# A gated mix of a two-dimensional spectral filter and a dense GELU layer on one core: output and dense sums in contiguous parts, operands at multiples of 256 bytes, first products reordered, four first folds by transfers, a new table of ranks

## The chip, the core and the metric

The kernel runs on one core of one Trainium2 chip. A core has a matrix engine (TensorE, PE in the profile, its weight loads PEld), a vector engine (VectorE, DVE), a scalar engine (ScalarE, ACT), GpSimd (POOL) and SyncE (SP). Transfers are issued by SP, ACT or POOL and all run on the same 16 DMA engines. The metric is device microseconds of one execution of the program; lower is better.

## The reference

```
x = A_x                                        # [1, 2048, 512] float32
g = sigmoid((x * gate_w).sum(-1))              # a gate for each of 2048 rows
X = rfft2(x) * (A_w_r + 1j * A_w_i)            # 2048 x 257 complex weights
a = irfft2(X)                                  # the spectral branch
h = gelu(x @ B_w1 + B_b1)                      # 512 -> 1792  (the rows of A_x are used for both branches)
b = h @ B_w2 + B_b2                            # 1792 -> 512
out = g * a + (1 - g) * b
```

In the last call of the reference both branches get `A_x`. All is float32.

## The kernel before

**Arithmetic.** Each float32 operand of a product is split into a high and a low part (`split`, L563 to L569: ACT rounds the high part, DVE subtracts it to get the low part), and one product is three matmuls, high by high, high by low, low by high (`prods`, L526). All matmuls, weight loads and transfers of the helpers show under the lines of the helpers: matmuls L524, transfers from POOL that add to their destination L515 (`acc`), plain ones from POOL L511 (`dma_pool`).

**Spectral branch.** The 2048 rows are 16 blocks `j` of 128. `forward(j)` folds the 512 columns into sums and differences (first folds L679, second folds L693), multiplies by a cosine and a sine table (`pd`), then by tables along the rows (`py`), and stores into the tile `y`. Four passes of radix-4 butterflies on DVE follow (`stage1`, `filt` with the weights `wf`, and `stage4`); `inverse(c, h)` multiplies by the inverse tables (`sw`, `pq`, `v`, `pz`, `z`), then by `ci` (`pa`), splits the result into sums and differences (`uv`, then `y`), and sends them to the output. The blocks of columns are called `c` = 0 to 3, halves of each `h` = 0, 1, and halves of the features `k` = 0, 1.

**Dense branch.** `mlp(half, c)` does for one block of 512 rows `c` one half of the hidden features: seven up products `ph` (12 matmuls of 512 columns each, weights `wa`), GELU on ACT, a split into `g_..h` and `g_..l`, and four down products `po` (weights `wb`). The first halves of the four sums go by SP to a DRAM tensor `bacc`; the second halves of c = 3, 0 and 1 are added there by POOL (L1121); the second half of c = 2 is joined on the chip (`bb`, `y<-bb`, `last`).

**Joining.** `combine(c, h)` loads a part of `bacc` by a plain POOL transfer into the tile `ba` (L1018), DVE multiplies it by gate minus one (L1023), and it is added to the output by POOL (L1029; for c = 1 it is written first by SP and `inverse` adds). So POOL's queue carries, in one order: additions to `bacc` (`bacc<-o`), loads `ba<-bacc`, additions to the output (`out<-uv`, `out<-y`, `out<-ba`), and `y<-bb`. For c = 3 and 0 each (c, h) has four additions to the output: `out<-uv`, `out<-y` and two `out<-ba`.

**Layout.** The output is `(4, P, NQ, 4, P)`: for one `(c, h, k)` each of 128 partitions has two runs of 1,024 bytes, 2,048 bytes apart. `bacc[c]` is `[P, NQ, 4, P]`. SBUF tiles of the pool `sb` are laid one behind the other in the order of their first use. The slots `xr` (made 2,056 bytes by the `wf` tile of 514 floats) and `ctab` (4,224 bytes) are no multiples of 256 bytes. So the weight slots of `wa0h`, `wa0l`, `wa1h`, `wa1l`, used later again by `wa7` and `wa8`, and the high and low x tiles `mxh`, `mxl` begin 32 bytes past a multiple of 256; `ctab` comes after them, and the weight slots from `wa2l` on (`wa3` to `wa6`, later `wa10` to `wa13`), all `wb` and all `g` begin 160 bytes past one.

**Order.** Every step (1,877 of them) is added to a graph with its reads and writes. A planner (`Graph.schedule`) runs a list schedule with a cost and a latency for each step; among the ready steps of an engine the lowest rank goes first, and a step also needs free slots of its buffers. Each engine then executes the planned order strictly in order: a step that waits holds all behind it on its engine. The ranks are a table of 1,877 numbers, `RANKS`, in hundredths of a microsecond of the planner's time; they behave as due times. The planner books 0.95 us of POOL for each transfer issued there and a latency; it has no limit on how many are under way. On the chip the POOL sequencer issues in order and sometimes sits before an issue with nothing to wait for that the profile shows ("issue" in its rows).

Of the kernel before, what the change touches and what calls it, by code (L numbers as in the profile page):

```python
# [17 lines left out]
P = 128  # L18
# [8 lines left out]
CW = 264  # L27
# [90 lines left out]
FOLD_DMA = 16  # L118
# [51 lines left out]
class Graph:  # L170
# [283 lines left out]
def tile_kernel(ctx: ExitStack, tc: tile.TileContext, xt, w1, w2, b1, b2, x0g, wf, wrev, out, consts):  # L454
# [50 lines left out]
    def dma(emit, kb, reads, writes, rank=FEED):  # L505
        out = not writes or any(b.pool is dp or b.name.startswith("out") for b in (w[0] if isinstance(w, tuple) else w for w in writes)
                                if not isinstance(b, View))
        return add("sp", kb / 300, 2.1 if out else 2.5, emit, reads, writes, rank)
# [740 lines left out]
```

## Time and profile before

| | us |
|---|---|
| Runs without the profiler, three | 409.2, 409.45, 411.6 (median 409.45) |
| The profiled execution, its own time | 410.21 |
| Its span, first to last instruction | 408.5 |
| PE busy | 376.5 (92%) |
| DVE busy | 327.4 (80%) |
| ACT busy | 228.1 (56%) |
| POOL busy | 63.6 (16%) |

The span is cut into what the engines were doing; 1.7 us of the profiled execution lie around it. A row of a timeline gives start, duration, engine, line, operation, out<-in, how many were merged, and in brackets the idle time of that engine just before it with what ended it. A row of the waits gives who waited for whom, the sum, how often, and the longest. A row of groups gives the busy time, the mean of one in ns, and the idle time before them. In a row of a stretch (A:B) each engine has its busy time and, as (x..), its instructions; behind them stand the granted TensorE clock as a share of full speed, the busy share of the DMA engines, and GB/s.

### The profile page before, as it was taken

What the parts mean: (1) busy time and instruction counts of PE and PEld (TensorE: products, weight loads), DVE (VectorE), ACT (ScalarE), POOL (GpSimd) and SP (SyncE); (2) the same over time, 40 slices, a digit from 0 to 9 for tenths busy, and PEclk for the clock granted to TensorE, in tenths of its full rate; (3) what the DMA queues carried; (4) which work ended last, traced back from release to release, by engine and by line L of the source; (5) the groups of instructions that cost most, each with busy time, mean ns of one, the idle gap of its engine ahead of it and who ended that gap; (6) DMA issues with size and microseconds to landing.
All of it is one profiled execution on the core that took longest, in us unless ns stands there. A gap on an engine that the chain in (4) does not pass through costs nothing. (4 is left out here: it accounts for less than half of the span.)

```text
span 408.5 us, 5587 instructions
## 1 busy us (share of the span) xinstructions
PE 376.5 (92%) x1839; PEld 315.2 (77%) x1839; DVE 327.4 (80%) x694; ACT 228.1 (56%) x454; POOL 63.6 (16%) x70
## 2 busy tenths in 40 slices
PE   8999999999999999999999999999678919998980
PEld 6888888888888888888888888888566808877880
DVE  5997999999997989899999977767253269589970
ACT  5756668766877354535651389479142077338600
POOL 0000000000000010211221110232431342333232
PEclk9999999999999999999999999999969966999996
DMA  8952889339543194774979331875569486465375
GB/s 260 372 149 77 238 281 319 119 105 293 179 121 90 20 236 103 173 172 121 264 133 267 53 52 35 273 131 79 102 132 281 79 137 101 75 106 145 88 141 90
DMA packets 51059, 63.23 MB, mean 155 GB/s; under 512 B 4720, under 2 KB 32944, under 8 KB 50256
## 3 DMA queue, kind: packets, MB, share of 16 engines
q1 hardware_dynamic: 39592, 46.37, 35.5%
q0 software_dynamic: 11296, 16.26, 26.2%
q8 instruction: 14, 0.23, 0.3%
q10 hardware_dynamic: 144, 0.26, 0.3%
q14 instruction: 13, 0.11, 0.1%
HBM read 38.62 MB, written 23.21 MB: 151 GB/s over the span
## 5 line engine op out<-in xcount | busy, mean ns | idle before, releaser
L1081 ACT ACTIVATE ph<-ph,b1t 128x512 f32<-128x512 f32 x56 | 36.8, 656 | 39.1 <-PE ph L524 38.3
L940 ACT ACTIVATE sw<-y,al 64x512 f32<-64x512 f32 x32 | 22.8, 720 | 15.2 <-DVE y L803 14.4
L1023 DVE SCALAR_TENSOR_TENSOR ba<-gb,ba 128x512 f32<-128x512 f32 x12 | 8.2, 687 | 28.3 <-DMA ba<-bacc 28.2
L515 POOL DMA_DIRECT2D wa7l<-in_w x1 | 1.0, 1037 | 144.3 <-PE po L524 144.3
L899 DVE TENSOR_TENSOR m<-y,wf 128x514 f32<-128x514 f32 x32 | 20.8, 688 | 0.2
L515 POOL DMA_DIRECT2D bacc<-o x12 | 11.9, 1019 | 43.4 <-ACT o L1120 40.8
L947 DVE SCALAR_TENSOR_TENSOR pq<-y,al,sw 128x256 f32<-128x256 f32 x32 | 14.4, 479 | 3.4 <-ACT sw L943 1.9
L1117 ACT ACTIVATE o<-po,b2t 128x512 f32<-128x512 f32 x16 | 11.0, 686 | 9.6 <-PE po L524 9.5
L1120 ACT ACTIVATE o<-po 128x512 f32<-128x512 f32 x12 | 7.1, 596 | 14.5 <-PE po L524 14.3
L515 POOL DMA_DIRECT2D out<-y x8 | 9.9, 1231 | 34.4 <-issue 16.0
L511 POOL DMA_DIRECT2D ba<-bacc x12 | 11.8, 981 | 18.7 <-DMA bacc<-o 9.2
L515 POOL DMA_DIRECT2D out<-ba x8 | 9.6, 1201 | 27.0 <-issue 9.3
L524 PE MATMUL pd<-cf,eoh 128*128 128x260 f32 x64 | 13.3, 294 | 0.0
L993 DVE TENSOR_TENSOR uv<-pa,od 128x512 f32<-128x512 f32 x16 | 10.5, 684 | 3.2 <-ACT od L990 3.1
L679 DVE TENSOR_TENSOR eo<-xr 128x256 f32<-128x256 f32 x30 | 12.1, 418 | 0.0
L524 PEld LDWEIGHTS pd<-cf,eoh 128*128 128x128 f32 x64 | 10.6, 189 | 1.9 <-issue 0.4
L755 ACT ACTIVATE y<-pys 64x257 f32<-64x257 f32 x24 | 9.9, 416 | 3.3 <-DVE pys L752 2.9
L990 ACT ACTIVATE od<-pa 128x512 f32<-128x512 f32 x8 | 4.8, 597 | 11.3 <-PE pa L524 11.2
L524 PE MATMUL pd<-cf,eol 128*128 128x130 f32 x64 | 10.4, 252 | 0.0
L943 ACT ACTIVATE sw<-y 1x512 f32<-1x512 f32 x16 | 10.1, 628 | 0.4
L524 PEld LDWEIGHTS pd<-cf,eol 128*128 128x128 f32 x64 | 9.9, 189 | 0.3
L524 PE MATMUL pz<-tg,v2h 128*128 128x256 f32 x4 | 1.5, 483 | 9.1 <-ACT v2h L567 9.1
(709 smaller groups left out, 1391.9 us busy)
## 6 DMA issues: line engine op xcount, KB each, us to landing
wf<-in_wf SPq DMA_DIRECT2D x16, 257.0 KB, 3.7
bacc<-o SPq DMA_DIRECT2D x16, 256.0 KB, 3.1
xr<-in_xt SPq DMA_DIRECT2D x15, 256.0 KB, 4.2
war<-in_w SPq DMA_DIRECT2D x14, 256.0 KB, 4.1
wbr<-in_w SPq DMA_DIRECT2D x14, 256.0 KB, 3.2
xm<-in_xt SPq DMA_DIRECT2D x12, 256.0 KB, 4.3
bacc<-o POOLq DMA_DIRECT2D x12, 256.0 KB, 5.2
ba<-bacc POOLq DMA_DIRECT2D x12, 256.0 KB, 4.1
```

The lines of the kernel that those rows point to most:

```text
L511: return add("pool", kb / 300, 3.2, lambda: nc.gpsimd.dma_start(dst(), src()), reads, writes, rank)
L515: return add("pool", kb / 150, 3.4, lambda: nc.gpsimd.dma_start(dst(), src(), accum_op=ALU.add), reads, writes, rank)
L524: pe.matmul(ps, w, x, start=start, stop=stop)
L679: v(lambda s=s, op=op: vec.tensor_tensor(eo.ap()[:, s], x.ap()[:, 0:2], x.ap()[:, 2:4], op=op), 256, [x], [(eo, s)], FEED)
L755: a(lambda o=o, i=i: act.activation(Y[j].ap()[o:o + HP, 1], pys.ap()[i:i + HP, 1], AF.Copy), 257, [(pys, 1)], [(Y[j], 1 + k)], 0, more=0.1)
L899: v(lambda mk=mk, k=k, y=y, w=w: vec.tensor_tensor(mk.ap(), y.ap(), w.ap()[:, k:k + 1, :ND].to_broadcast([P, 2, ND]), op=ALU.mult), 514, [ ...
L940: a(lambda sw=sw, y=y, o=o, i=i: act.activation(sw.ap()[o:o + HP], y.ap()[i:i + HP, ::-1, :HD], AF.Copy, scale=al.ap()[i:i + HP, 0:1]), 51 ...
L943: a(lambda sw=sw, y=y, j=j: act.activation(sw.ap()[HP:HP + 1], y.ap()[HP:HP + 1, ::-1, :HD], AF.Copy, scale=math.cos(math.pi * j / NJ)), 5 ...
L947: v(lambda sw=sw, pq_=pq_, y=y, j=j, k=k, op=op: vec.scalar_tensor_tensor(pq_.ap()[:, k], y.ap()[:, k, :HD], al.ap()[:, 1 + j:2 + j], sw.a ...
L993: v(lambda i=i, op=op: vec.tensor_tensor(uv.ap()[:, i], ps.ap()[:, 0], od.ap(), op=op), 512, [ps, od], [(uv, i)], 2)
L1081: a(lambda f=f, ps=ps: act.activation(ps.ap(), ps.ap(), AF.Gelu_apprx_tanh, bias=b1t.ap()[:, f:f + 1]), 600, [b1t], [ps], 0.9 if half else ...
L1117: a(lambda o=o, ps=ps, q=q: act.activation(o.ap(), ps.ap(), AF.Identity, scale=-1.0, bias=b2t.ap()[:, q:q + 1]), 600, [b2t, ps], [o])
```

## The change

1. **Contiguous parts.** The output becomes `(4, 2, 2, P, 2, 2 * P)`, so that a part `(c, h, k)` is one contiguous block with one run of 2,048 bytes for each partition. `bacc[c]` becomes `[NQ, P, 4 * P]`. The host's final transposition follows. The `last` step of c = 2 now writes two runs of 1,024 bytes for each partition. On the SBUF side `ba` and `o` have 2,048 contiguous bytes for each partition; `uv[:, :, 1]` and `y[:, :, :256]` have two runs of 1,024 bytes, before and after.
2. **Alignment.** `CW` 264 to 272 (the `ctab` slot becomes 4,352 bytes), the `wf` tile 257 to 288 columns (the `xr` slot becomes 2,304 bytes), `b1t` moves into the pool `sa`. All tiles of the pool `sb` then begin at multiples of 256 bytes. `ti` has 3 slots instead of 4.
3. **First products.** For the first up product the order of the three kinds becomes high by high, low weights by high x, high weights by low x; the second column half waits for the first; the first weight tile is rounded on DVE instead of ACT; 11 warming matmuls instead of 12.
4. **Folds by transfers.** `FOLD_DMA` 16 to 12: for the last four blocks in `NORD` (j = 3, 7, 11, 15) the two DVE operations of the first fold are replaced by a load, a negation of half of it on ACT (256 columns) and an adding POOL transfer of the same block with its halves exchanged; the second folds on DVE then read that.
5. **New ranks**, and other latencies in the planner for the first loads.

```diff
-CW = 264
+CW = 272
-FOLD_DMA = 16
+FOLD_DMA = 12
-"so": 2, "ba": 2,  "pf": 2, "pm": 4, "ti": 4}
+"so": 2, "ba": 2,  "pf": 2, "pm": 4, "ti": 3}
-    b1t = one("b1t", [P, NF])
+    b1t = one("b1t", [P, NF], pool=sa)
-    bacc = [one(f"bacc{c}", [P, NQ, 4, P], pool=dp, parts=2 * NQ) for c in range(4)]
+    bacc = [one(f"bacc{c}", [NQ, P, 4 * P], pool=dp, parts=2 * NQ) for c in range(4)]
...
-        a(lambda: act.activation(h.ap(), view(src.ap()), AF.Copy), n, [src], [h], rank)
+        if fast:
+            v(lambda: vec.tensor_copy(h.ap(), view(src.ap())), n, [src], [h], rank)
+        else:
+            a(lambda: act.activation(h.ap(), view(src.ap()), AF.Copy), n, [src], [h], rank)
...
-        for _ in range(12):
+        for _ in range(11):
             mm(none.ap(), zero.ap(), bcast(zero.ap(), 4), True, True)
...
-            w = buf("xr", [P, 2, ND], F32, f"wf{k2}")
+            w = buf("xr", [P, 2, 288], F32, f"wf{k2}")
...
     def part(c, h, k):
-        return out[c][:, 2 * k:2 * k + 2, 2 * h:2 * h + 2].rearrange("p a b c -> p a (b c)")
+        return out[c][h, k]
...
-            dma_pool(lambda b=b: b.ap(), lambda k=k: bacc[c].ap()[:, 2 * k:2 * k + 2, 2 * h:2 * h + 2].rearrange("p a b c -> p a (b c)"),
+            dma_pool(lambda b=b: b.ap(), lambda k=k: bacc[c].ap()[2 * k:2 * k + 2, :, 2 * h * P:(2 * h + 2) * P].rearrange("q p n -> p q n"),
...
-                    for z, (k, l) in enumerate(((0, 0), (0, 1), (1, 0))):
+                    for z, (k, l) in enumerate(((0, 0), (1, 0), (0, 1))):
...
-        dma(lambda: sp.dma_start(out[c][:, q].rearrange("p a b -> p (a b)")[:, n], o.ap()[:, n]),
+        dma(lambda: sp.dma_start(out[c][hs[0]:hs[-1] + 1, q // 2, :, q % 2].rearrange("h p n -> p h n"),
+                                 o.ap()[:, n].rearrange("p (h n) -> p h n", n=2 * P)),
...
-_OUTS = [((4, P, NQ, 4, P), "float32")]
+_OUTS = [((4, 2, 2, P, 2, 2 * P), "float32")]
```

Some entries of `RANKS`, here divided by 100, that the prediction speaks of. "Load" is the rank of `ba<-bacc` on POOL, "use" that of DVE's L1023 on the same tile; the digits are k, c, h.

| step | before | after |
|---|---|---|
| first addition to `bacc` of c = 0 | 255.66 | 255.15 |
| last group of matmuls of the program | 379.03 | 376.56 |
| ba031: load, use | 269.47, 282.38 | 257.14, 280.88 |
| ba131: load, use | 271.19, 284.82 | 259.20, 278.87 |
| ba000: load, use | 288.19, 293.40 | 286.24, 290.65 |
| ba100: load, use | 292.27, 299.16 | 288.28, 302.67 |
| ba001: load, use | 301.68, 309.89 | 296.77, 308.19 |
| ba101: load, use | 309.65, 314.91 | 309.72, 317.94 |
| ba010: load, use | 322.76, 329.21 | 315.98, 339.48 |
| ba110: load, use | 339.59, 343.92 | 326.99, 341.09 |
| ba011: load, use | 338.51, 347.15 | 335.74, 354.49 |
| ba111: load, use | 347.55, 357.75 | 342.29, 356.45 |
| last two `out<-y` of c = 1 | 367.43, 368.07 | 369.51, 370.46 |
| j = 3: adding transfer, second fold, last split, first `pd` | no transfer | 67.15, 72.58, 76.75, 81.75 |

More of the change, by code (lines that the diff above doesn't have):

```diff
@@ L503, in m, with dma @@
         return add("pe", c_pe(n, k), 0.25, emit, reads, writes, rank)
-    def dma(emit, kb, reads, writes, rank=FEED):
+    def dma(emit, kb, reads, writes, rank=FEED, first=None):
+        if first is not None:
+            return add("sp", kb / 390, first, emit, reads, writes, rank)
         out = not writes or any(b.pool is dp or b.name.startswith("out") for b in (w[0] if isinstance(w, tuple) else w for w in writes)
@@ L517, in dma_act @@
     def dma_act(emit, kb, reads, writes):
-        return add("act", 0.4, kb / 300 + 2.7, emit, reads, writes, 0)
+        return add("act", 0.4, kb / 390 + 2.9, emit, reads, writes, 0)
     def raw(dst, src, q=sp):
@@ L578, in load_x @@
         x = buf(tag, [P, NQ, P], F32, f"x{tag[1:]}{j}")
-        dma(lambda: sp.dma_start(x.ap(), xt[j]), 512 if j == NORD[1] else 256, [], [x], j / 100 if tag == "xr" and j in NORD[:4] else rank)
+        dma(lambda: sp.dma_start(x.ap(), xt[j]), 512 if j == NORD[1] else 256, [], [x], j / 100 if tag == "xr" and j in NORD[:4] else rank, 2.45 if j in NORD[:4] else None)
         return x
@@ L589, in warm @@
     def warm():
-        for _ in range(12):
+        for _ in range(11):
             mm(none.ap(), zero.ap(), bcast(zero.ap(), 4), True, True)
-    add("pe", 5.2, 0.1, warm, [zero], [none], 0)
+    add("pe", 4.75, 0.1, warm, [zero], [none], 0)
     x0 = buf("z", [P, NQ + 1, P], F32, "xf0")
@@ L1038, in load_w @@
         t = buf("wr" + n, [P, D], F32, f"w{n}r{f}")
-        dma(lambda: sp.dma_start(t.ap(), (w1 if n == "a" else w2)[f]), 256, [], [t], early(n, f, 0.05) if f < FA else 2)
+        dma(lambda: sp.dma_start(t.ap(), (w1 if n == "a" else w2)[f]), 256, [], [t], early(n, f, 0.05) if f < FA else 2, None if n == "b" or f > 3 else 2.45 if f else 3.1)
         if f < FA:
-            W[n, f] = split(f"w{n}{f}", "w" + n, [P, D], t, lambda x: x, 512, early(n, f, EARLY - 0.1))
+            W[n, f] = split(f"w{n}{f}", "w" + n, [P, D], t, lambda x: x, 512, early(n, f, EARLY - 0.1), n == "a" and f == 0)
             return
@@ L1074, in some @@
                                last and q == NQ - 1)
-                    for z, (k, l) in enumerate(((0, 0), (0, 1), (1, 0))):
+                    for z, (k, l) in enumerate(((0, 0), (1, 0), (0, 1))):
                         m(lambda k=k, l=l, z=z, some=some: some(k, l, z == 0, z == 2), 256, 4,
-                          [W["a", f][k], *((xx[l], 2 * n + i) for i in range(2))], [(ps, n)])
+                          [W["a", f][k], *((xx[l], 2 * n + i) for i in range(2)), *((ps, i) for i in range(n))], [(ps, n)])
             else:
@@ L1093, in mlp @@
                 b = buf("wra", [P, 4 * P], F32, f"bb{c}{q}")
-                dma(lambda b=b, q=q: sp.dma_start(b.ap(), bacc[c].ap()[:, q].rearrange("p a b -> p (a b)")), 256,
+                dma(lambda b=b, q=q: sp.dma_start(b.ap(), bacc[c].ap()[q]), 256,
                     [(bacc[c], 2 * q), (bacc[c], 2 * q + 1)], [b], 3)
@@ L1120, in mlp @@
                 a(lambda o=o, ps=ps: act.activation(o.ap(), ps.ap(), AF.Copy, scale=-1.0), 512, [ps], [o], 2)
-                acc(lambda q=q: bacc[c].ap()[:, q].rearrange("p a b -> p (a b)"), lambda o=o: o.ap(), 256, [o],
+                acc(lambda q=q: bacc[c].ap()[q], lambda o=o: o.ap(), 256, [o],
                     [(bacc[c], 2 * q), (bacc[c], 2 * q + 1)], 4)
             if half == 0:
-                dma(lambda o=o, q=q: sp.dma_start(bacc[c].ap()[:, q].rearrange("p a b -> p (a b)"), o.ap()), 256, [o],
+                dma(lambda o=o, q=q: sp.dma_start(bacc[c].ap()[q], o.ap()), 256, [o],
                     [(bacc[c], 2 * q), (bacc[c], 2 * q + 1)], 4)
@@ L1244 @@
     y = np.empty((P, NJ, D), np.float32)
-    o = np.asarray(r.results[0]["out_0"]).transpose(4, 3, 0, 2, 1).reshape(P, NJ, D)
+    o = np.asarray(r.results[0]["out_0"]).reshape(4, 2, 2, P, 2, 2, P).transpose(6, 1, 5, 0, 2, 4, 3).reshape(P, NJ, D)
     y[:, :, DORD] = o
```

220 rows, old and new, of the table RANKS are left out of this document.

## The prediction

> **What bounds the kernel now.** I read the page first, then the waits of PE, then stretches around its two long waits, then the timelines of DVE and of POOL.
>
> ```profile
> PE 376.5 (92%) x1839; PEld 315.2 (77%) x1839; DVE 327.4 (80%) x694; ACT 228.1 (56%) x454; POOL 63.6 (16%) x70
> PE   8999999999999999999999999999678919998980
> PEclk9999999999999999999999999999969966999996
> PE pz L524 <- ACT v2h L567: 9.1, 1, 9.1
> PE pz L524 <- DVE uv L993: 6.3, 1, 6.3
> PE ph L524 <- DVE g_10l L568: 2.0, 1, 2.0
> PE po L524 <- DVE g_12l L568: 1.3, 1, 1.3
> 298.40:302.60 4.20, 4.14 (x14) 3.69 (x15) 2.73 (x7) 3.01 (x7) 1.20 (x1) 0.50 0.87 194
> 336.40:343.70 7.30, 7.24 (x24) 6.29 (x25) 6.78 (x13) 6.82 (x14) 1.47 (x2) 0.50 0.67 112
> 398.20:408.50 10.30, 0.00 (x0) 0.00 (x0) 0.57 (x2) 0.00 (x0) 2.62 (x3) 0.67 0.57 89
> ```
>
> PE is full for the first 290 us, so there only fewer or faster matmuls help. After that it loses four waits, 18.7 us together, and behind the two long ones the granted clock is 0.50 for 4.2 and 7.3 us, which costs half of 11.5, 5.75 us. The last 10.3 us hold no matmul. Some 35 of 408.5 us are thus not matmul at full speed, nearly all late.
>
> Who makes PE wait? The named releasers are DVE or an ACT step behind it, so DVE's own waits come next, and then the queue that feeds them.
>
> ```profile
> DVE ba L1023 <- DMA ba<-bacc: 28.2, 4, 8.4
> 323.91 0.69 DVE L1023 SCALAR_TENSOR_TENSOR ba<-gb,ba 128x512 f32<-128x512 f32 x1 [8.31 <-DMA ba<-bacc]
> 262.08 0.88 POOL L515 DMA_DIRECT2D bacc<-o  x1 [20.81 <-ACT o L1120]
> 269.18 1.20 POOL L515 DMA_DIRECT2D out<-y  x1 [4.71 <-issue]
> 269.92 1.38 POOL L515 DMA_DIRECT2D bacc<-o  x1
> 273.99 1.21 POOL L515 DMA_DIRECT2D out<-ba  x1 [2.69 <-issue]
> 278.32 1.20 POOL L515 DMA_DIRECT2D out<-ba  x1 [3.12 <-issue]
> 287.79 1.21 POOL L515 DMA_DIRECT2D out<-uv  x1 [3.29 <-issue]
> 288.52 1.24 POOL L511 DMA_DIRECT2D ba<-bacc  x1
> 292.48 0.75 POOL L511 DMA_DIRECT2D ba<-bacc  x1 [2.72 <-issue]
> 293.22 1.85 POOL L515 DMA_DIRECT2D bacc<-o  x2
> 367.99 1.49 POOL L511 DMA_DIRECT2D ba<-bacc  x2 [4.99 <-issue]
> 403.15 1.20 POOL L515 DMA_DIRECT2D out<-y  x1 [3.53 <-issue]
> bacc<-o POOLq DMA_DIRECT2D x12, 256.0 KB, 5.2
> ba<-bacc POOLq DMA_DIRECT2D x12, 256.0 KB, 4.1
> out<-y POOLq DMA_DIRECT2D x8, 256.0 KB, 4.3
> out<-ba POOLq DMA_DIRECT2D x8, 256.0 KB, 4.3
> ```
>
> Four times DVE stands before L1023, in all 28.2 us, with the radix and `pq` steps that PE needs queued behind it. The load it waits for stands in POOL's queue, and POOL is slow in a particular way: an addition to the output is issued only about when the one before has landed (4.3 us), so they follow each other by some 4.5 us. An addition to `bacc` goes out at once behind one of them (269.92). One `ba<-bacc` fits behind one (288.52), the second waits (292.48) until the first addition has landed at about 292.1, and then three lighter ones are under way together. I infer a limit on what is under way: an addition to the output counts as two, everything else as one, and at most three fit. So 20 additions of 4.5 us make 90 us of a queue that runs from 262 to 403.
>
> Beside the table of ranks: the first addition to `bacc` of c = 0 is due at 255.66 and is issued at 262.08, 6.4 late; the load ba011 is due at 338.51 and issued at 367.99, 29.5 late. The queue, not PE, lost those 23 us in between.
>
> **The change part by part.** *The parts of the output.* What makes an addition to the output count double? I take the rows of two stretches that each hold one addition of 256 KB, `out<-ba` in 278.5 to 283 and `bacc<-o` in 230 to 236:
>
> ```profile
> q0 software_dynamic: 272, 0.26, 43.9%
> q0 software_dynamic: 144, 0.26, 36.2%
> ```
>
> 272 packets against 144: 256 runs of 1,024 bytes against 128 of 2,048, with 16 more each. Both occupy the engines alike (0.439 of 4.5 us is 2.0; 0.362 of 6 us is 2.2). So longer runs do not shorten a transfer; they can only make it count less. That happens where both sides have runs of 2,048 bytes: the eight `out<-ba`, and not the four `out<-uv` and eight `out<-y`, whose SBUF side stays in runs of 1,024 bytes. I take it so; the other end is that the output side alone decides and all 20 get light. A group of four for one (c, h) is now 4 times 4.5, 18 us. After: `out<-uv` at 0, `out<-y` at 4.5, the first `out<-ba` behind it at 5.7, the second when `out<-y` lands at 8.9, the next group from about 10.5. That saves 7.5 us in each of four groups, 30 us of queue time against 23 lost: the queue stays near its due times. `bacc` in contiguous blocks keeps its 2,048 byte runs; the loads keep theirs: nothing. `out<-o` gets runs half as long; five such transfers; all but the last lie beside matmuls, and the last may cost up to 1 us, which is inside the term for the end.
>
> By the Trainium skill, page "DMA: Bandwidth & Descriptors", section Specifications, runs of 512 bytes and more already reach the line rate, so by that rule parts in longer runs bring nothing. The occupied times above agree with it, and what I book is not transfer but the wait between issues; by the rule alone the result is that of the second rival.
>
> *The new ranks.* From the due time of a load to that of L1023 the old table leaves 5.2, 7.0, 8.2 and 5.3 us (ba000, ba100, ba001, ba101), then 6.5 and 4.3 (ba010, ba110); with 4.1 from issue to landing, a queue 5 us late stops DVE. The new one leaves 4.4, 14.4, 11.4, 8.2, 23.5 and 14.1, and 23.7 and 19.7 instead of 12.9 and 13.6 for ba031 and ba131, where DVE stood for 7.9 us. Only ba000 stays tight. So both the queue and the table take away DVE's four waits. What is late next is the table's own idleness. It spans 121.4 us from the first addition of c = 0 to the last group of matmuls (255.15 to 376.56). The trace has 136.1 (262.08 to 398.2).
>
> ```profile
> 260.00:400.00 140.00, 118.41 (x595) 99.78 (x593) 92.78 (x180) 67.52 (x117) 44.91 (x45) 0.93 0.64 124
> ```
>
> Of PE's 118.4 us, 2.1 lie ahead of 262.08 and 5.75 are the slow clock: 110.6 us of work at full speed, so the new table still leaves 10.8 us of PE idle. DVE's 92.8 us of work fit into 121 too. I take the table as reached: 136.1 less 121.4, **14.7 us gained**. Bounds: 7, half of the waits return; 25, all of waits and slow clock go.
>
> The Trainium skill, page "TensorE: Matmul & The Clock Gate", Part 1, has the clock halve after some 3.4 us of idle PE. The trace agrees: 0.50 behind the waits of 6.3 and 9.1 us, 1.00 behind that of 2.0. By it the 10.8 us cost nothing more if they come in short pieces, and up to some 5 us more if in two.
>
> *Alignment.* Up products with different weight slots take different times, whatever the moment:
>
> ```profile
> L524 PE MATMUL ph<-mxh,wa1l 128*128 128x512 f32 x16 | 6.2, 390 | 0.0
> L524 PE MATMUL ph<-mxl,wa7h 128*128 128x512 f32 x16 | 6.2, 390 | 0.0
> L524 PE MATMUL ph<-mxh,wa6l 128*128 128x512 f32 x16 | 6.3, 394 | 0.0
> L524 PE MATMUL ph<-mxl,wa13h 128*128 128x512 f32 x16 | 6.3, 394 | 0.0
> ```
>
> The slots of `wa0`, `wa1`, `wa7`, `wa8`, at 32 bytes past 256, take 390 ns in the rows shown, the others, at 160 past, 394, with the same x tiles. Of 672 up matmuls some 500 are of the slower kind: 500 times 4 ns, 2 us; the down products (390 to 410 in their rows) may give as much. Bounds: nothing, if another property of the slot is the cause; 4.6. I take **3 us**; two thirds of it lies where PE is full.
>
> *First products.*
>
> ```profile
> 1.06 5.22 PE L524 MATMUL none<-zero 128*128 128x512 f32 x12 [1.06 <-DVE zero L584]
> PE ph L524 <- DVE mxl L641: 0.8, 1, 0.8
> ```
>
> One warming matmul less is 0.4 us, and the wait of 0.8 for `mxl` may go as low weights come first. But the first weight's rounding moves to DVE, which is in the same chain. Between 0 and 1.2: **0.5 us**.
>
> *Folds by transfers.*
>
> ```profile
> L679 DVE TENSOR_TENSOR eo<-xr 128x256 f32<-128x256 f32 x30 | 12.1, 418 | 0.0
> 60.00:90.00 30.00, 30.00 (x166) 26.00 (x165) 28.28 (x72) 22.64 (x62) 0.00 (x0) 1.00 0.59 184
> wb9l<-in_w POOLq DMA_DIRECT2D x1, 256.0 KB, 8.1
> ```
>
> Eight DVE steps of 418 ns, 3.3 us, leave a DVE that is 94% busy there; PE is full, so that gains nothing. Four negations on ACT (22.6 of 30 us busy) and four loads of 256 KB are hidden. New is a wait: the second fold on DVE waits for the adding transfer, and behind it in DVE's order stand the splits of other products. For j = 3 the table leaves 5.4 us, and additions land after 5.2, at worst 8.1; then 5.0 us lie between the last split and the first `pd`. So DVE may stand 2.7 us per fold while PE goes on. POOL is idle until 144, so nothing stands behind them there. Cost: nothing to 11 us; I take **1**.
>
> *End.* The last `out<-y` are issued at 398 and 403 because the queue is late and they go one by one. The table has them at 369.5 and 370.5, ahead of the last matmuls. Two heavy additions 6 us late still end some 6 us behind the last matmul: **4 us** of 10.3, between 0 and 6. `ti` with three slots: its small loads lie beside matmuls; if one came late, its landing would stand before a `pz`, within the bounds of 14.7.
>
> *Left over.* Twelve additions stay heavy and the tight ba000 stays: 2 us against it.
>
> **The sum.** 14.7 + 3 + 0.5 − 1 + 4 − 2 = 19.2. The profiled execution took 410.21 us for a span of 408.45, 1.76 around it: 408.45 − 19.2 + 1.76 = **391 us**. It stands 0.8 above the median of 409.45, within the runs shown.
>
> **The rivals.**
>
> 1. *The queue stays the bound.* Twelve of 20 additions keep their weight, and the four of c = 1 and `y<-bb` still go one by one at the end. For it: `out<-y` of the last stretch is not touched. Against: the 23 us were lost in the groups that get lighter. Half of 14.7 and no gain at the end: 7.3 + 3 + 0.5 − 1 = 9.8, **400 us**.
> 2. *It does not do what it says*: the wait between issues hangs on order, not on runs, and the ranks only move DVE's waits elsewhere. Alignment alone: **407 us**. Against it: a lighter transfer goes out at once behind a heavy one, a heavy one never.
> 3. *Slower, by the folds.* The load, ACT's negation and the addition are a chain that DVE holds all others for. The 16 DMA engines were busy 0.59 of 60 to 90. If each addition landed 16 us after its issue, twice the slowest, DVE would stand 10.6 us each time and PE, after 5.0 of slack, 5.6 and again some 2 at half clock: 4 times 7.6, 30 us against 19 gained, **421 us**. It decides from a landing of some 13 us on. Nothing in the trace lands so late, and the folds come in a stretch without any other POOL transfer.
>
> **How the numbers follow.** My forecast gets 0.72, the first rival 0.14, the second 0.08, the third 0.06. Lower end of the range: 14.7, alignment at 4.6, the end at 6, the start at 1.2, nothing against, and a little of the table's idleness filled: 27, 383. Upper end: 7 of the 14.7, nothing for alignment and end, 0.5 at the start, 1 for the folds: 6.5 and thus 404, which holds the first rival as well; outside lie the second and the third. Chances against 409.45, with 1% the least that these runs can tell from no change (409.2 to 411.6 is 0.6% alone): faster than 405.4 in 0.84, within in 0.10, slower in 0.06.
>
> **What would show it.** POOL: two `out<-ba` close together, packets of `out<-ba` at 144 instead of 272, the load ba011 less than 15 us behind its rank. DVE's wait for `ba<-bacc` under 10 us instead of 28.2. PE: no wait over 6 us after 290, clock 1.00 there. All `ph` groups at 390 ns. Less than 7 us after the last matmul. I am wrong if DVE still stands before L1023, if PE waits for a `pd` or its splits between 60 and 110, or if the up products keep two speeds.

## The result, and the profile after

The changed kernel takes **392.56 us** (median of four runs, 390.0 to 393.76) against 410.11 for the kernel before in the same comparison: a ratio of 0.956, with a 95% interval of 0.950 to 0.962. The forecast was 391 us with a range of 383 to 404. The profiled execution took 392.12 us for a span of 390.4.

The page of the kernel after: busy time by engine, and PE and its granted clock in 40 slices.

```profile
PE 370.8 (95%) x1838; PEld 313.5 (80%) x1838; DVE 325.9 (84%) x687; ACT 229.7 (59%) x457; POOL 64.5 (17%) x74
PE   8999999998999999999999999999978999999980
PEclk9999999998999999999999999999996999999995
```

Waits of the kernel after (engine, line, what it waited for: us in total, times, longest):

```profile
PE pz L526 <- DVE uv L998: 4.9, 2, 4.4
PE pd L526 <- DVE x3l L735: 1.7, 1, 1.7
DVE ba L1028 <- DMA ba<-bacc: 7.9, 2, 6.0
DVE cl L698 <- DMA eo<-in_xt: 2.7, 1, 2.7
```

The table by stretches of the kernel after (PE, PEld, DVE, ACT, POOL busy, then granted clock, DMA share, GB/s):

```profile
90.00:95.00 5.00, 3.13 (x18) 2.51 (x17) 4.16 (x10) 2.73 (x8) 0.00 (x0) 0.97 0.64 165
95.00:100.00 5.00, 5.00 (x21) 4.10 (x20) 3.73 (x11) 3.58 (x11) 0.00 (x0) 0.69 0.92 278
290.00:300.00 10.00, 5.74 (x19) 4.94 (x20) 7.34 (x16) 5.33 (x11) 3.83 (x5) 0.66 0.90 179
300.00:330.00 30.00, 30.00 (x154) 25.58 (x153) 22.60 (x46) 20.56 (x34) 8.06 (x10) 1.00 0.84 179
379.20:390.40 11.20, 0.00 (x0) 0.00 (x0) 0.84 (x2) 0.00 (x0) 2.79 (x3) 0.60 0.57 83
```

DVE's 28.2 us in front of its multiplication by gate minus one (L1023, now L1028) have become 7.9. Of PE's four late waits of over a microsecond one is left, 4.4 us, with its half clock behind it (0.66 in 290 to 300). One loss is new: PE stands for 1.9 us in 90 to 95 and runs at 0.69 behind it. The kernel before did not lose that:

```profile
90.00:100.00 10.00, 10.00 (x53) 8.54 (x52) 9.71 (x22) 7.09 (x18) 0.00 (x0) 1.00 0.95 267
```

One loss stays: the last 11.2 us hold no matmul, as 10.3 did before.

POOL's queue after, in order of time (start, us, what was issued; in brackets the idle time before it):

```profile
81.52 1.21 POOL L517 DMA_DIRECT2D eo<-in_xt  x1 [3.83 <-DVE x14l L734]
86.30 1.23 POOL L517 DMA_DIRECT2D eo<-in_xt  x1 [3.57 <-DVE y L754]
259.15 0.87 POOL L517 DMA_DIRECT2D bacc<-o  x1 [21.91 <-ACT o L1125]
266.99 1.09 POOL L517 DMA_DIRECT2D out<-uv  x1 [4.74 <-DVE uv L998]
271.82 1.77 POOL L517 DMA_DIRECT2D out<-ba  x2 [2.85 <-issue]
280.97 1.09 POOL L517 DMA_DIRECT2D out<-uv  x1 [3.53 <-DVE z00l L975]
281.58 1.24 POOL L513 DMA_DIRECT2D ba<-bacc  x1
285.79 0.76 POOL L513 DMA_DIRECT2D ba<-bacc  x1 [2.97 <-issue]
354.55 0.75 POOL L513 DMA_DIRECT2D ba<-bacc  x1 [3.11 <-DVE pq L952]
379.56 1.33 POOL L517 DMA_DIRECT2D out<-y  x1
384.34 1.10 POOL L517 DMA_DIRECT2D out<-y  x1 [3.45 <-issue]
```

Two `out<-ba` go out as a pair at 271.82, where before they stood 4.3 us apart. An addition that kept runs of 1,024 bytes still has no second such addition beside it, and at most one other transfer: the last two `out<-y` are 4.8 us apart; behind `out<-uv` at 280.97 one load goes out at 281.58, and the next waits until 285.79. That second load is what DVE waits 6.0 us for.

### The profile page after: what moved, and what is told of

The parts are those of the page before. It is cut to its first block, busy times and chain, and to the rows that moved or that the text cites. A ratio compares the mean times of both kernels' runs of the same rounds, so it can differ in the third digit from the quotient of the medians.

```text
span 390.4 us, 5587 instructions
## 1 busy us (share of the span) xinstructions
PE 370.8 (95%) x1838; PEld 313.5 (80%) x1838; DVE 325.9 (84%) x687; ACT 229.7 (59%) x457; POOL 64.5 (17%) x74
## 4 chain that ended last, share of the span: by engine, by line
PE 70%; DMA 8%; issue 8%; DVE 7%; POOL 3%; ACT 3%; POOLq 0%; SPq 0%; DVEq 0%; ACTq 0%
PE ph L526 31%; PE po L526 30%; PE pz L526 3%; PE pd L526 2%; PE py L526 2%; POOL out L517 2%; DMA eo<-in_xt 2%; DMA ba<-bacc 2%; PE pa L526 2%; DMA out<-uv 1%; DVE uv L998 1%; DMA xr<-in_xt 1%; DMA tf<-tf 1%; ACT ph L1086 1%; DVE y L763 0%
## 5 line engine op out<-in xcount | busy, mean ns | idle before, releaser
L517 POOL DMA_DIRECT2D eo<-in_xt x4 | 5.0, 1256 | 82.1 <-DMA tf<-tf 67.6
L517 POOL DMA_DIRECT2D bacc<-o x12 | 11.2, 983 | 38.7 <-ACT o L1125 35.8
L1125 ACT ACTIVATE o<-po 128x512 f32<-128x512 f32 x12 | 7.0, 594 | 17.1 <-PE po L526 10.2
L1028 DVE SCALAR_TENSOR_TENSOR ba<-gb,ba 128x512 f32<-128x512 f32 x12 | 8.2, 686 | 7.9 <-DMA ba<-bacc 7.9
L513 POOL DMA_DIRECT2D ba<-bacc x12 | 10.0, 835 | 24.7 <-DMA bacc<-o 10.0
L517 POOL DMA_DIRECT2D out<-y x8 | 9.0, 1128 | 27.9 <-DVE y L1009 11.0
L517 POOL DMA_DIRECT2D out<-ba x8 | 7.7, 1000 | 12.1 <-DVE ba L1028 7.2
L517 POOL DMA_DIRECT2D y<-bb x8 | 7.6, 954 | 11.0 <-DVE y L1009 6.2
```

The lines of the kernel that those rows point to most:

```text
L513: return add("pool", kb / 300, 3.2, lambda: nc.gpsimd.dma_start(dst(), src()), reads, writes, rank)
L517: return add("pool", kb / 150, 3.4, lambda: nc.gpsimd.dma_start(dst(), src(), accum_op=ALU.add), reads, writes, rank)
L1028: vec.scalar_tensor_tensor(b.ap(), gg, 1.0, b.ap(), op0=ALU.subtract, op1=ALU.mult)
```

## The experiments

Theory: POOL's transfers share a small room. A transfer holds its part from issue to landing; an addition with runs of 1,024 bytes on a side ("heavy") holds about twice what one with 2,048 on both ("light") holds; the kernel before loses its time in waiting for room. Rivals: the new table of ranks moved the waits away; longer runs are a faster transfer; a heavy addition waits for another reason, such as order on the output.

Times below are medians; each ratio is to the kernel before, run on the same chip in the same comparison, with its 95% interval. "Order unchanged" means that every engine issues the same steps in the same order.

### Layout alone, and everything but the layout

`b_layout` is the kernel before with this edit, and `a_oldlayout` the kernel after with it undone:

```diff
-    bacc = [one(f"bacc{c}", [P, NQ, 4, P], pool=dp, parts=2 * NQ) for c in range(4)]
+    bacc = [one(f"bacc{c}", [NQ, P, 4 * P], pool=dp, parts=2 * NQ) for c in range(4)]
...
-        return out[c][:, 2 * k:2 * k + 2, 2 * h:2 * h + 2].rearrange("p a b c -> p a (b c)")
+        return out[c][h, k]
...
-_OUTS = [((4, P, NQ, 4, P), "float32")]
+_OUTS = [((4, 2, 2, P, 2, 2 * P), "float32")]
```

> The kernel before with the new layout of output and dense sums alone; old table of ranks, order of steps unchanged. Theory (queue lost 23 us against the table, and lighter out<-ba give most of them back): two out<-ba close together, DVE's four waits of 28.2 us fall below 15 us, 397 to 403 us. Rival (the table alone made the gain): DVE's waits stay above 22 us, 407 to 411 us.

> The kernel after, with output and dense sums laid out as before; table of ranks, folds, alignment and first products as after, order of steps unchanged. Theory (the lighter out<-ba carry about half of the gain on the queue): 272 packets for each out<-ba, four additions of a group one by one 4.5 us apart, DVE's wait for ba<-bacc back above 15 us, 398 to 403 us. Rival (the table alone moved the waits away): 391 to 394 us although the queue runs later. Second rival (both needed, neither does anything alone): 405 to 408 us, as before less the alignment.

Measured: `b_layout` 395.56 us (394.43 to 398.0), ratio 0.964 (0.960 to 0.969); `a_oldlayout` 405.79 us (405.08 to 409.12), ratio 0.990 (0.987 to 0.994). The waits, first of `b_layout`, then of `a_oldlayout`:

```profile
DVE ba L1023 <- DMA ba<-bacc: 14.4, 3, 8.3
PE pz L524 <- ACT v2h L567: 5.7, 1, 5.7
```

```profile
DVE ba L1028 <- DMA ba<-bacc: 23.7, 5, 11.6
PE pz L526 <- DVE uv L998: 12.3, 2, 10.0
```

The layout alone brings 14.8 of the 17.6 us, under the old table. The new table, alignment, folds and first products together bring 4.6 without it, and DVE's wait stays at 23.7. So the table did not move the waits away. `a_oldlayout` came out 2.8 us above the range that the theory gave and inside that of its second rival (both parts needed, neither works alone); `b_layout` excludes that rival, and what failed is the size: the layout weighs more than I had given it. `b_layout` itself came out 1.4 us below its range, for the same reason.

### Making the other twelve additions light

`a_light` gives `out<-y` and `out<-uv` a contiguous SBUF side (order unchanged):

```diff
+    def flat(b):
+        return b.ap().rearrange("p a n -> p (a n)")[:, :4 * P].rearrange("p (a n) -> p a n", a=2)
...
-            acc(lambda: part(c, h, 0), lambda: uv.ap()[:, :, 1], 256, [uv], [(OUT[c], 2 * h)], 4)
+            acc(lambda: part(c, h, 0), lambda: uv.ap()[:, 1], 256, [uv], [(OUT[c], 2 * h)], 4)
...
-                acc(lambda k=k: part(c, h, k), lambda w=w: w.ap()[:, :, :2 * P], 256, [w], [(OUT[c], 2 * h + k)], 4)
+                acc(lambda k=k: part(c, h, k), lambda w=w: flat(w), 256, [w], [(OUT[c], 2 * h + k)], 4)
```

> The kernel after, with the last twelve additions to the output (four out<-uv, eight out<-y) given an SBUF side of 2,048 contiguous bytes per partition as well; order of steps unchanged. Theory (an addition counts two on POOL's queue only while one of its sides is in runs of 1,024 bytes, and the queue also sets the end): all out<-y and out<-uv show 144 packets instead of 272, the last two out<-y are issued within 1.5 us of their data (377 us) instead of at 379.56 and 384.34, the stretch behind the last matmul shrinks from about 11.4 to about 6.5 us, DVE's wait before L1028 stays below 8 us: 384 to 388 us. Rival A (every addition to the output counts two whatever its runs, and the table alone made the gain): packets change, the issues stay 4.6 us apart, 391 to 394 us. Rival B (the end hangs on the landing of out<-o): POOL's issues move and the time does not, 391 to 394 us.

Measured: **378.62 us** (377.03 to 379.64), ratio 0.922 (0.919 to 0.925), 14 us under the changed kernel. The end of POOL's queue in `a_light`; the packets, MB and share of the software queue from 367 us on; and the stretch behind its last matmul:

```profile
368.29 1.77 POOL L517 DMA_DIRECT2D out<-y  x2 [2.55 <-DVE y L1009]
```

```profile
q0 software_dynamic: 432, 0.66, 49.6%
```

```profile
370.30:376.50 6.20, 0.00 (x0) 0.00 (x0) 0.42 (x1) 0.00 (x0) 0.00 (x0) 0.75 0.64 117
```

The last two `out<-y` go out as a pair when DVE has written them. The 432 packets are three additions of 144 (two `out<-y`, and a `y<-bb` still under way). The tail is 6.2 us instead of 11.2. The time is well under the 384 to 388 us expected, since DVE's waits for `ba<-bacc` went altogether, and with them PE's late wait. Rivals A and B fall.

### The room itself

The program declares a scratch for POOL's transfers. Three kernels change only its size (order unchanged in the first two; `b_ring` also has `ti` in three slots to make room, which lets the planner place some steps elsewhere):

```diff
-    nc = bacc.Bacc("TRN2", target_bir_lowering=False, num_devices=1, dynamic_dma_scratch_size=1024)
+    nc = bacc.Bacc("TRN2", target_bir_lowering=False, num_devices=1, dynamic_dma_scratch_size=1472)
```

> The kernel after with nothing changed but the size of the scratch that the program declares for POOL's transfers, 1,472 instead of 1,024 bytes. Theory (the limit on what is under way is room in that scratch, where a heavy addition takes twice the room of a light one): two heavy additions go out within 1.5 us of each other (out<-y behind out<-uv, and the out<-y of the end), the stretch behind the last matmul shrinks from 11.4 to about 6.5 us, 384 to 389 us. Rival (a heavy addition waits for the one before it to land for another reason, say its order on the output): issues still 4.6 us apart, 391 to 394 us.

> The kernel after with the scratch at 1,088 instead of 1,024 bytes and nothing else changed; where does the room for a second heavy addition begin? In 1,024 bytes one heavy and one light transfer stood side by side, three light ones did, two heavy ones never, nor one heavy and two light. Theory (a heavy addition takes a little over half of 1,024 bytes, since a light one takes about a third and two heavy ones just fail): 64 bytes more let two heavy ones out together, 376 to 380 us. Rival (a heavy one takes clearly more, say two thirds): heavy ones still 4.6 us apart, 390 to 394 us.

> The kernel before with the scratch for POOL's transfers at 2,048 instead of 1,024 bytes, and ti in three slots instead of four, which makes the room; everything else as before (old layout, old table, no alignment). Theory (the whole of the queue's loss is room in that scratch; the rest of the change is worth alignment 3.4, table 2 and the first products some 0.5): 376.4 + 6 = 382 us (380 to 385), additions to the output within 1.5 us of each other, DVE's wait for ba<-bacc below 6 us. Rival (the layout and the table are needed as well): 390 us or more.

Measured: `a_ring1472` **376.38 us** (376.22 to 377.16), ratio 0.917 (0.915 to 0.920); `a_ring1088`, 64 bytes more than the changed kernel, 376.96 us (376.19 to 377.51), ratio 0.917 (0.914 to 0.920); `b_ring`, the kernel before with 2,048 bytes, 381.34 us (379.71 to 383.51), ratio 0.928 (0.924 to 0.933). The queue of `a_ring1472` and three of its stretches, then the queue of `a_ring1088`, and DVE's wait in `b_ring`:

```profile
81.50 2.47 POOL L517 DMA_DIRECT2D eo<-in_xt  x2 [3.90 <-DVE x14l L734]
256.06 0.86 POOL L517 DMA_DIRECT2D bacc<-o  x1 [21.72 <-ACT o L1125]
257.84 1.08 POOL L517 DMA_DIRECT2D out<-y  x1 [0.91 <-DVE ti L936]
258.99 1.10 POOL L517 DMA_DIRECT2D out<-uv  x1
366.25 2.21 POOL L517 DMA_DIRECT2D out<-y  x2 [2.31 <-DVE y L1009]
```

```profile
90.00:95.00 5.00, 4.74 (x26) 3.62 (x25) 5.00 (x12) 4.94 (x13) 0.00 (x0) 1.00 0.85 244
256.00:368.20 112.20, 112.20 (x600) 96.69 (x598) 92.61 (x178) 67.52 (x116) 41.69 (x46) 1.00 0.77 155
368.20:374.70 6.50, 0.00 (x0) 0.00 (x0) 0.42 (x1) 0.00 (x0) 0.27 (x1) 0.88 0.70 119
```

```profile
257.40 0.88 POOL L517 DMA_DIRECT2D bacc<-o  x1 [22.21 <-ACT o L1125]
259.12 1.09 POOL L517 DMA_DIRECT2D out<-y  x1 [0.84 <-DVE ti L936]
262.19 1.10 POOL L517 DMA_DIRECT2D out<-uv  x1 [1.98 <-issue]
359.94 2.31 POOL L517 DMA_DIRECT2D out<-y  x2 [10.76 <-DVE y L1009]
```

```profile
DVE ba L1023 <- DMA ba<-bacc: 0.9, 1, 0.9
```

With room, heavy additions go out as pairs, and PE is busy for all of the 112.2 us from the first addition of c = 0 to the last matmul. `a_ring1472` came out 8 us below the range expected, since the folds and the late wait of PE turned out to hang on room as well; `a_ring1088` and `b_ring` came out inside theirs. 64 bytes decide it: two heavy additions do not fit in 1,024 and do in 1,088, so each takes over 512 and at most 544 bytes, if both take the same. With a light one under way as well (`bacc<-o` at 257.40 in `a_ring1088`) the second heavy one still waits, until 262.19; in 1,472 bytes it goes at 258.99. By the Trainium skill, page "DMA: Bandwidth & Descriptors", section Terms, a descriptor has 16 bytes and POOL's path writes them to rings in SBUF. By the Trainium skill, page "Collectives: The Full Stack", Part 3, the add of a reduce step needs two source reads, so two read descriptors for each chunk. An estimate from both: 16 pieces per engine make 32 reads and one descriptor to finish, 528 bytes; 8 pieces make 272. Pairs of 528 fail at 1,024 and fit at 1,088, as measured; three of 272 fit in 1,024 and 528 with two of 272 (1,072) does not, as the queue shows. In 1,088 bytes the 1,072 should fit, and they do: the heavy addition that `a_ring1088` issued at 262.19 landed after 4.1 us, and before that two light ones went out beside it:

```profile
264.52 0.88 POOL L517 DMA_DIRECT2D bacc<-o  x1 [1.23 <-ACT o L1125]
265.08 1.22 POOL L517 DMA_DIRECT2D out<-ba  x1
```

In the changed kernel, with 1,024 bytes, `out<-ba` behind the same two (266.99 and 267.56) waited until 271.82. No run here counts descriptors.

### Layout, once there is room

`r_oldlayout` is `a_ring1472` with the old layout, `r_light` is `a_ring1472` with `a_light`'s edit (order unchanged in both).

> The kernel after with the scratch of 1,472 bytes, and output and dense sums laid out as before. Theory (the layout does nothing but take less room in the scratch): with room for two heavy additions the old layout costs little, DVE's wait for ba<-bacc below 6 us, packets of out<-ba at 272, 376.5 to 381 us instead of the 405.79 that it gave with 1,024 bytes. Rival (longer runs or contiguous parts are worth something of themselves): 385 us or more.

> The kernel after with both the scratch of 1,472 bytes and the twelve remaining additions in runs of 2,048 bytes on both sides (a_light and a_ring1472 together). Theory (both do the same thing, make room; once there is room the other adds nothing): 376 to 377 us. Rival (shorter transfers or fewer waits at three in flight still count): below 375.5 us.

Measured: `r_oldlayout` 376.82 us (376.63 to 377.3), ratio 0.918 (0.914 to 0.922); `r_light` 376.14 us (376.08 to 377.14), ratio 0.916 (0.913 to 0.919). Three layouts, one time. Longer runs are worth nothing here but the room that they leave, which agrees with the rule on 512 byte runs that the prediction quoted from the Trainium skill. That rule still gave the wrong time (407 us), because transfer was not what the layout saved.

### The rest of the change, with the queue out of the way

Each undoes one part of `a_ring1472`: `r_noalign` the alignment (order unchanged), `r_oldranks` the table together with the folds, `r_nofold` the folds, `r_nofirst` the first products. In the last three the planner also places other steps differently, so they bound a part and do not isolate it.

```diff
-CW = 272
+CW = 264
-    b1t = one("b1t", [P, NF], pool=sa)
+    b1t = one("b1t", [P, NF])
-            w = buf("xr", [P, 2, 288], F32, f"wf{k2}")
+            w = buf("xr", [P, 2, ND], F32, f"wf{k2}")
```

> The kernel after with the scratch of 1,472 bytes (a_ring1472, 376.38 us), and the alignment undone: constants table 264 wide, wf tile 257, b1t back in its old pool; order of steps unchanged. With the queue roomy the runs are steady, so a small term shows. Theory (weights that start at 160 past a multiple of 256 cost 4 ns a matmul, most of it where PE is full): the up products of those slots back at 393 to 398 ns, 378.5 to 381 us. Rival (the 4 ns are absorbed, or belong to something else): 375.7 to 377.2 us.

> The kernel after with the scratch of 1,472 bytes, and the old table of ranks, which goes with the four folds on DVE; layout, alignment and first products as after. Theory (with a roomy queue the old table's tight loads, 4.3 and 5.2 us ahead of their use, still stop DVE now and then): DVE's waits for ba<-bacc 3 to 8 us, 378 to 384 us. Rival A (all of the table's worth was the queue's lateness): 375.5 to 377.5 us. Rival B (the table is worth much by itself): 386 us or more.

> The kernel after with the scratch of 1,472 bytes, and the four folds back on DVE, under the new table of ranks; the planner then puts the steps of all engines in somewhat other places, so this run bounds the folds and does not isolate them. Theory (folds by transfers cost about 1 us of waits for the adding transfer and save nothing, since PE is full there): 374.5 to 377 us, no wait of DVE for eo. Rival (DVE's 3.3 us are worth something): 378 us or more.

> The kernel after with the scratch of 1,472 bytes, and the first products undone: twelve warming matmuls, products in the old order, the first weight rounded on ACT. Theory (worth 0.5 us, between 0 and 1.2): 376.4 to 377.6 us. Rival (the wait in the first microseconds only moves): 375.9 to 376.5 us.

Measured: `r_noalign` 379.82 us (379.27 to 381.19), ratio 0.924 (0.919 to 0.929); `r_oldranks` 378.45 (377.63 to 380.41), 0.922 (0.917 to 0.927); `r_nofold` 378.0 (376.55 to 378.51), 0.920 (0.915 to 0.924); `r_nofirst` 377.04 (376.49 to 377.51), 0.918 (0.915 to 0.921). The costliest groups (busy, then mean ns of one) of the up products, first of `r_noalign`, then of `a_ring1472`:

```profile
L526 PE MATMUL ph<-mxh,wa6l 128*128 128x512 f32 x16 | 6.3, 395 | 0.0
L526 PE MATMUL ph<-mxl,wa13h 128*128 128x512 f32 x16 | 6.3, 395 | 0.0
```

```profile
L526 PE MATMUL ph<-mxh,wa6l 128*128 128x512 f32 x16 | 6.2, 390 | 0.0
L526 PE MATMUL ph<-mxl,wa13h 128*128 128x512 f32 x16 | 6.2, 390 | 0.0
```

Alignment is worth 3.0 us against `r_oldlayout`, which ran on the same chip and whose runs do not overlap with it. The table with the folds comes to 2.1 against `a_ring1472`, and to 1.6 against `r_oldlayout`, on the same chip and without overlap. `r_oldranks` has no wait of DVE for `ba<-bacc`, so the reason that I gave (tight loads) fell, and what these 2 us come from is open. The folds come to 1.6, on the rival's side, the first products to 0.7. The runs of these two overlap with those of `r_oldlayout` and `r_light`, which ran beside them on the same chips: they are not told from nothing.

## Why the prediction was right

The time was right to 1.6 us, and the main mechanism, the parts of the output, was right. That it came so close is luck: terms of the sum were wrong by 10 us and more and cancelled. Set out as stretches of the span:

| stretch | predicted gain | measured | us before and after |
|---|---|---|---|
| up to the first addition of c = 0 | 2 + 0.5 − 1 = 1.5 | 2.9 | 262.08 to 259.15 |
| from it to the last matmul | 14.7 + 1 − 2 = 13.7 | 16.1 | 136.1 to 120.0 |
| behind the last matmul | 4 | −1.0 | 10.2 to 11.2 |
| sum | 19.2 | 18.0 | 408.45 to 390.4 |

**The parts of the output: right, and the main term.** Heavy counts two, light one, three fit: `b_layout`, `a_light` and the three sizes of the scratch bear out both the count and that both sides need long runs. The prediction called this an inference; `a_ring1472` and `a_ring1088` show it.

**The new ranks: credit misplaced.** That "both the queue and the table take away DVE's four waits" failed: the table without the layout leaves 23.7 us of waits there. The table's share, with the folds, is about 2 us.

**"The table's own idleness": wrong.** I put 10.8 us of idle PE down to the table. With room there is none: 112.2 of 112.2 us busy. What is due 121.4 us apart in the table is done in 112.1 (256.06 to 368.2), so a table of ranks is an order, not a clock. The gain that was there is 136.1 − 112.1 = 24.0, close to the upper bound of 25.

**"Left over": sized at 2, measured at 14 to 16.** The twelve heavy additions still cost the changed kernel 392.56 − 378.62 = 13.9 us by `a_light`. Want of room costs it 16.2 by `a_ring1472`, which also frees the folds; in `a_light` DVE still waits 2.3 us for them. Most of it can be found in the changed kernel's own trace: 4.4 us of wait up to 294.3 and half of some 5.2 us of work at half clock behind it, 7.0; at the end 11.2 against 6.5, 4.7; at the folds 1.9 us and 0.31 of 5 us, 3.4; 15.1 in all. This term and the one before it were wrong by about as much, in opposite directions.

**End: failed.** I took `out<-y` to be issued near their ranks. DVE wrote the last two by 377.4, but they stood behind heavy ones and went out at 379.56 and 384.34. With room the tail is 6.5 us, and the sign "less than 7 us" is met there.

**Folds: right in sign, the cause was missed.** "Nothing stands behind them there" was wrong: they stand behind each other. The fourth addition was issued 4.8 us after the third, at 86.30, where `a_ring1472` issues both at once; DVE then waited 2.7 us and PE stood for 1.9 in 90 to 95; with the slow clock behind it that is 3.4 us, not 1. The third rival's price (a landing of 13 us) never came near; the DMA issues of the kernel after have the median landing last:

```profile
eo<-in_xt POOLq DMA_DIRECT2D x4, 256.0 KB, 4.5
```

**Alignment: right.** 3 us forecast, 3.0 measured, the slow groups back at 395 ns. **First products:** 0.5 forecast, 0.7 measured, which is not told from nothing.

**Signs.** Met: pairs of `out<-ba`, DVE's wait at 7.9, no late wait of PE over 6 us. Missed: the load ba011 is 18.8 us behind its rank (354.55 against 335.74) instead of under 15; the clock is 0.66 in 290 to 300; the tail. Of the three things named as showing it wrong, two came in part: DVE still stands before L1028 for 7.9 us, and PE waits 1.7 us for a split ahead of a `pd` at 91 to 93. The third did not: `ph<-mxl,wa13h`, 394 ns before, takes 390. The first rival ("the queue stays the bound") had the mechanism of what was left; only its time of 400 us was too high.

Split by room, with the ratios taken on 410.1 us: more room is worth 29.4 us to the kernel before (`b_ring`, 380.7) and 15.9 to the changed one (376.2 against 392.1). So of 18.0 us the change won 13.5 back from the queue, and 4.5 elsewhere; the single undoings give 3.0, 2.1 and 0.7 for that, 5.8, which the intervals (1 to 2 us each) allow. **The fastest kernels are `r_light`, 376.14, and `a_ring1472`, 376.38 us**, not to be told apart, both 4% under the changed kernel.

## What to carry to other kernels

Where one engine's transfers are issued only when an earlier one lands, while lighter ones slip past, look for a shared room before changing layouts or order: here 64 bytes more of it did at least as much as making every addition to the output light (376.96 and 378.62 us), and enlarging it brought the old kernel more than the whole change. A table of due times is an order; do not read idle time out of it. When several terms of a sum hang on one queue, ask for each user of that queue what it still waits for, the new users (the folds) too.

## What the hardware showed that was not expected

- The room that an addition takes depends on its runs: two of 256 runs of 1,024 bytes need more than 1,024 and at most 1,088 bytes of scratch; with enough room the kernel's time does not differ (three layouts, 376.1 to 376.8 us), and longer runs do not land sooner (`out<-y`: a median of 4.6 us in `r_oldlayout`, 5.0 in `r_light`).
- The granted clock can halve after a shorter wait than the 2.0 us that left it at 1.00 in the kernel before. In the changed kernel PE stood still for 1.74 us, ran again, and was then at half clock for about three microseconds (four of the rows from 91 to 98):

```profile
91.00:92.00 1.00, 0.00 (x0) 0.00 (x0) 1.00 (x3) 0.37 (x2) 0.00 (x0) 1.00 0.56 184
93.00:94.00 1.00, 1.00 (x8) 0.91 (x7) 1.00 (x3) 0.80 (x2) 0.00 (x0) 1.00 0.75 147
95.00:96.00 1.00, 1.00 (x4) 0.81 (x3) 1.00 (x4) 0.58 (x3) 0.00 (x0) 0.50 1.07 318
97.00:98.00 1.00, 1.00 (x4) 0.85 (x3) 1.00 (x4) 0.96 (x3) 0.00 (x0) 0.50 0.57 164
```

  The Trainium skill, page "TensorE: Matmul & The Clock Gate", Part 1, has the clock halve after some 3.4 us of idle PE; this wait was half of that. In all of 90 to 95 PE stood for 1.87 us, hardly more than this one wait. What else counts stays open.
- The start of a weight tile sets the time of a matmul: 390 ns against 395 for the same product, by its place alone. Why is not shown.
